# Issuing every engine in source order from the third token chunk on, in a one-core attention and feed-forward kernel

## The chip, the cores and the metric

The kernel runs on one core of a Trainium2 chip. The metric is the device time of one launch in microseconds. Four compute engines work beside each other: PE (matrix products), DVE (vector), ACT (scalar functions and scaled copies) and POOL (a second, slower vector engine). SP starts the DMA transfers. Each engine executes its own instruction list in order, and semaphores join the lists.

## The reference

Linear attention with random features for 8 batches of 576 tokens and 8 heads, then a feed-forward layer on the 4608 tokens that come out:

```python
def _attn_ref(q, k, v, omega):
    m, D = omega.shape                       # 128 features, head_dim 64
    scale = 1.0 / np.sqrt(np.sqrt(D))
    q_s, k_s = (q * scale, k * scale)
    def phi(x):
        proj = np.einsum('bhsd,md->bhsm', x, omega)
        sq = np.sum(x * x, axis=-1, keepdims=True) / 2.0
        h = proj - sq
        h = h - np.max(h, axis=-1, keepdims=True)
        return np.exp(h) / np.sqrt(m)
    q_p, k_p = (phi(q_s), phi(k_s))
    kv = np.einsum('bhsm,bhsd->bhmd', k_p, v)
    z = np.sum(k_p, axis=2)
    num = np.einsum('bhsm,bhmd->bhsd', q_p, kv)
    den = np.einsum('bhsm,bhm->bhs', q_p, z)[..., None] + 1e-06
    return num / den

def _moe_ref(x, w_in, w_out):                # x 4608x512, w_in 512x2048, w_out 2048x512
    h = x @ w_in
    sp = np.where(h > 20.0, h, np.log1p(np.exp(np.minimum(h, 20.0))))
    g = h * np.tanh(sp)                      # Mish
    return g @ w_out
```

## The kernel before

**Numbers.** Nearly every factor is held as two fp16 parts, the rounded value (hi) and what is left of it (lo), and a product is three products: lo·hi, hi·lo and hi·hi. The function cast makes hi, mostly on ACT (L72), and the function rest makes lo, on DVE (L81, L83) or POOL (L81).

**Work.** The 4608 tokens make 18 chunks (c) of 256. Three kinds of work stand beside each other:

- *The feed-forward layer.* ff_in(c) forms h = x·w_in in PSUM (tile ph, L689), eight steps ("i") of 24 matmuls 128x256. ACT applies Mish (L834), ACT makes hi of g and DVE lo (L83). ff_out(c-1) forms g·w_out (tile po, L858), eight steps ("o") of 12 matmuls 128x512. ACT copies po to the tile o, and SP stores it.
- *Query units,* two a chunk (q_task): SP loads fq. ACT makes hi of it (tile sq) and POOL lo. PE projects it (pq, L340). DVE takes the maximum and subtracts it (mxq L349, eq L358). ACT applies Exp and makes hi of qn, and DVE lo. SP transposes qn to qp. PE multiplies by kv (pn, L495), DVE divides (rd, x) and casts (xs), POOL makes lo of xs, and SP transposes xs into the chunk's tile xT, the right factor of ff_in.
- *Key units,* four a batch (k_task): the same as far as Exp, with fk, sk, pk, mxk, ek and kp; then PE multiplies kp by the values vb (pkv, L445). The values of a whole batch are loaded by v_task as four tiles vf. DVE takes their largest magnitude (vmx L278), which scales them.

The functions of ACT lie in two tables, one for Exp and one for Mish. Each change of function is an ACT_TABLE_LOAD.

**Chunks 15 to 17** (SC0 = 15) use seven block products in place of eight (ff_in7). Four of the seven left factors are sums of blocks of w_in (s1 to s4). The function s_make forms them ahead of that, once for each of four quarter pairs ("sets"): DVE adds fp16 blocks into an fp32 tile s (L724), ACT makes hi (L72), DVE lo (L81), and SP writes the pair to DRAM. ff_in7 loads them back (w<-ds), and DVE joins the products (L801).

**Order.** A step counter (slot) drives generators. From chunk 2 on a slot is one "i" or one "o" step of the feed-forward layer, followed by whatever the agenda has due: each `yield n` in a unit sets it back by n slots. Chunk c begins at slot 65 + 16(c-2). Units start by the hand list FIRST (18 entries) and then by pace(c), a linear rule. The source order made in this way isn't what the engines execute: a scheduler orders each engine's list by its own model, and an instruction written late may stand early. The sets start at slots 211, 222, 233 and 244 and take eight slots each.

**Buffers** that the prediction speaks of: three xT tiles, two xs, five vf, five ht (the h tiles and the tile s of s_make).

Of the kernel before, what the change touches and what calls it, by code (L numbers as in the profile page):

```python
# [9 lines left out]
F16 = mybir.dt.float16  # L10
# [20 lines left out]
def tile_kernel(  # L31
# [58 lines left out]

    idle = const.tile([P, 512], F16, name="idle")
    dve.memset(idle, 1.0)
# [34 lines left out]
    def pow2(amax, tag, top):  # L127


        allm = over_partitions(amax, tag)  # L130
# [12 lines left out]

    NB = 8
    BW = KT * DF // NB
    wo_t = const.tile([P, NB, 2, BW], F16, name="wo")
    slots = [const.tile([P, 2, BW], F16, name=f"w{i}") for i in range(NB + 1)]
    slots += [wo_t[:, i] for i in range(NB)]
    def flat32(slot):
# [121 lines left out]
    def v_task(b):  # L271
# [117 lines left out]
    def k_task(nth, b, hp):  # L389
# [75 lines left out]
    def q_task(nth, t):  # L465
        c, off = t * P // CH, t * P % CH
        if c not in xT:
            xT[c] = sb.tile([P, 2, KT, CH], F16, tag="xT", name=f"xT{c}", bufs=3)
        rows = slice(0, P)
# [13 lines left out]
        )  # L483
        yield 2
        x = sb.tile([P, H, D], F32, tag="x", name=f"x{t}", bufs=2)
# [31 lines left out]

    x_more = {}

    def x_region(c, r):  # L520

        n = (4, 4, 4, 2)[r]
        if r < 2:
            return xT[c].rearrange("p a k s -> p (a k s)")[:, r * 1024:(r + 1) * 1024].rearrange(
                "p (a k s) -> p a k s", a=2, k=n
            )
        if (c, r) not in x_more:
            x_more[c, r] = sb.tile([P, 2, n, P], F16, tag="vf", name=f"xm{c}_{r}", bufs=5)
# [36 lines left out]
    def x_parts(nth, t, x):  # L565
        c, off = t * P // CH, t * P % CH
        if c >= SC0:
            yield from x_sums(nth, t, x)
            return
        xs = sb.tile([P, 2, H * D], F16, tag="xs", name=f"xs{t}", bufs=2)  # L570
# [4 lines left out]
        nc.sync.dma_start_transpose(  # L575
            out=xT[c].rearrange("p a k s -> p (a k) s")[:, :, off:off + P],
            in_=xs.rearrange("p a c -> p (a c)"),
        )
        did("x", c)
# [90 lines left out]
    def ff_in(c):  # L670
# [3 lines left out]
        for gr in range(FT // FG):  # L674
            gT[c, gr] = sb.tile([P, 2, FG, CH], F16, tag="g", name=f"g{c}_{gr}", bufs=GB)
            for q in range(FG // FQ):
# [4 lines left out]
                for j in range(0, FQ, 2):  # L681
                    ph = ps_h.tile([P, 2, CH], F32, tag="h", name=f"ph{c}_{gr}_{q}_{j}")
                    for i in range(2):
# [4 lines left out]
                        for n, (a, y, k) in enumerate(mm):  # L688
                            nc.tensor.matmul(  # L689
                                out=ph[:, i, :], lhsT=wi(a, k, f) if c else wi0(k, f),  # L690
                                rhs=xT[c][:, y, k, :] if c else xT0()[:, k, :],
                                start=n == 0, stop=n == len(mm) - 1,
# [16 lines left out]

    SUMS = ("s2", "s3", "s1", "s4")  # L710
    sums = {}
# [4 lines left out]
    def s_make(gr, hb):  # L716
# [18 lines left out]
        tt(s, s, u, ALU.add)  # L735
        send("s1", s)
        yield 2
        tt(s, s, block(sl1, 0, 0))
        tt(s, s, block(sl1, 1, 0))
        send("s2", s)  # L740
        yield 2
        tt(u, block(sl1, 0, 1), s)
        tt(u, u, block(sl1, 1, 1), ALU.add)
        send("s4", u)
        yield 2
# [3 lines left out]
        send("s3", s)  # L749
        did("sums")  # L750
# [15 lines left out]
    def ff_in7(c):  # L766
# [18 lines left out]

        def products(gr, op_l, op_r):
            r, k0 = right[op_r]
            mm = [(a, y, k) for a, y in ((1, 0), (0, 1), (0, 0)) for k in range(2)]
            ph = ps_a.tile([P, FQ, P], F32, tag="a", name=f"p_{op_l}_{c}_{gr}")
            for i in range(FQ):  # L790
                for n, (a, y, k) in enumerate(mm):
                    nc.tensor.matmul(  # L792
                        out=ph[:, i, :], lhsT=left(gr, op_l, i, a, k), rhs=x_region(c, r)[:, y, k0 + k, :],
                        start=n == 0, stop=n == len(mm) - 1,
                    )
            if op_l in SUMS:
                ask_sum()
            return ph

        def add(out, in0, bank):  # L800
            dve.tensor_tensor(out=out, in0=bank, in1=in0, op=ALU.add)  # L801

        for gr in range(FT // FG):
# [4 lines left out]

            p1 = products(gr, "a11", "b11")
            cast(act, c21, p1)  # L810
            yield
            add(c11, c21, products(gr, "a12", "b21"))
            yield
            add(c12, c21, products(gr, "s2", "t2"))
            yield
            add(c21, c12, products(gr, "s3", "t3"))
            yield
            p5 = products(gr, "s1", "t1")
            add(c22, c21, p5)
            add(c12, c12, p5)  # L820
            yield
            add(c12, c12, products(gr, "s4", "b22"))
            later(1, mish, sp, h[0], h[0])
            later(2, g_split, c, gr, 0, sp, h[0])
            yield
            add(c21, c21, products(gr, "a22", "t4"))
            later(1, mish, sp, h[1], h[1])
            later(2, g_split, c, gr, 1, sp, h[1])
            yield

# [89 lines left out]

    def pace(c):

        return 15 + (c - 1) * 4.0 if c < 5 else 31.0 + (c - 5) * 3.8

# [37 lines left out]

    items, need = [], {}
    nb = 0
    for t in range(NT):
        last = (t * P + P - 1) // S
        while nb <= last:
            items += [("k", nb, hp) for hp in range(HP)]
            nb += 1
        items.append(("q", t))  # L970
        need[t * P // CH] = len(items)
    given = [0]

    def give():
        if given[0] < len(items):
            it = items[given[0]]
            given[0] += 1
            start((k_task if it[0] == "k" else q_task)(given[0] - 1, *it[1:]))
            if it[0] == "k" and it[2] == HP - 1 and it[1] + 1 < B:
                start(v_task(it[1] + 1), V1)  # L980

    w_in_v = w_in.rearrange("(k p) f -> p k f", p=P)
# [14 lines left out]
    for what in PREL.split():  # L997
# [58 lines left out]
    while agenda:  # L1056
        step()


# [39 lines left out]
```

## Time and profile before

Three runs took 983.06, 964.0 and 962.81 us, a median of 964.0 us.

| | |
|---|---|
| profiled execution: time | 962.69 us |
| its span | 960.8 us |
| mean granted TensorE clock | 0.992 |
| busy PE, ACT, DVE, POOL over the span | 98%, 66%, 65%, 23% |
| 192 to 264 us: PE busy of 72 us | 70.84 |
| 264 to 624 us: PE, ACT, DVE busy of 360 us | 359.57, 263.90, 219.69 |
| 624 to 768 us (sets of s_make): PE, ACT, DVE busy of 144 us | 140.03, 111.36, 121.17 |
| 816 to 936 us (seven products): PE, ACT, DVE busy of 120 us | 120.00, 37.88, 50.91 |

In the profile's lines an instruction is `start us, length us, engine, line, operation, out<-in, shape, xcount`, and a bracket holds the idle time ahead of it and what ended that. Lengths on one engine overlap a little: the next instruction can begin shortly before the end of the last. Chunk 2 begins near 190 us. The first 190 us load and split the weights, and the last 24 us are the last chunk's output product.

### The profile page before, as it was taken

The numbers are of one execution on the slowest core, as the hardware profiler recorded it, in microseconds if no ns is written. First come the engines' busy times: TensorE is split into PE (matmuls) and PEld (weight loads), VectorE is DVE, ScalarE is ACT, GpSimd is POOL, SyncE is SP. The second block draws the span as 40 slices with busy tenths as digits, with TensorE's granted clock in tenths as the row PEclk, the third lists the DMA queues.
The fourth block names the chain that finished last, engine by engine and source line by source line (L and its number), as shares of the span: only waits on it lengthen the run. The fifth ranks groups of instructions, "written<-read, shape, count | busy, mean of one in ns | idle before, by whom it ended". The sixth has DMA issues, their size and how long they took to land. (4 is left out here: it accounts for less than half of the span.)

```text
span 960.8 us, 20397 instructions
## 1 busy us (share of the span) xinstructions
PE 940.9 (98%) x8568; PEld 679.3 (71%) x8568; DVE 624.9 (65%) x1080; ACT 633.9 (66%) x818; POOL 222.7 (23%) x141
## 2 busy tenths in 40 slices
PE   9999988999999999999999999999989999999998
PEld 6788873677677777777777777777756777777663
DVE  5879797587766666656575655788889656643330
ACT  4758875686877877768667775778776866332231
POOL 0000052242432322322133333222231332200000
PEclk9979999999999999999999999999999999999999
DMA  9866314431741346313431253423552145634410
GB/s 287 271 208 208 109 48 94 102 58 61 140 92 37 107 77 119 69 59 75 101 68 53 69 118 66 93 89 68 136 124 73 37 100 115 172 117 131 133 57 33
DMA packets 147403, 100.25 MB, mean 104 GB/s; under 512 B 112112, under 2 KB 124528, under 8 KB 147312
## 3 DMA queue, kind: packets, MB, share of 16 engines
q1 hardware_dynamic: 147312, 98.95, 41.2%
q8 instruction: 67, 1.10, 0.5%
q14 instruction: 24, 0.20, 0.1%
HBM read 58.95 MB, written 13.63 MB: 76 GB/s over the span
## 5 line engine op out<-in xcount | busy, mean ns | idle before, releaser
L858 PE MATMUL po<-wo,g 128*128 128x512 f16 x1632 | 375.2, 380 | 0.0
L689 PE MATMUL ph<-xT,w 128*128 128x256 f16 (+1 forms) x2816 | 344.8, 279 | 0.7 <-ACT xT L72 0.7
L689 PEld LDWEIGHTS <-w 128*128 128x128 f16 x2688 | 261.0, 98 | 47.3 <-issue 0.7
L858 PEld LDWEIGHTS <-g 128*128 128x128 f16 x1632 | 155.1, 98 | 163.9 <-issue 2.2
L83 DVE SCALAR_TENSOR_TENSOR g<-h,us,g 128x1024 f16<-128x1024 f32 (+3 forms) x92 | 120.2, 1316 | 36.8 <-ACT g L72 36.2
L834 ACT ACTIVATE h<-ph,us 128x512 f32<-128x512 f32 (+3 forms) x152 | 83.3, 573 | 77.6 <-PE ph L689 76.8
L81 POOL TENSOR_TENSOR sq<-fq,sq 64x1024 f16<-64x1024 f32 x31 | 69.0, 2227 | 159.1 <-issue 65.2
L81 POOL TENSOR_TENSOR sk<-fk,sk 64x1152 f16<-64x1152 f32 x24 | 60.5, 2520 | 111.5 <-ACT sk L72 86.9
L81 POOL TENSOR_TENSOR xs<-x,xs 128x512 f16<-128x512 f32 (+1 forms) x35 | 44.2, 1264 | 151.9 <-issue 68.0
L72 ACT ACTIVATE g<-h,us 128x1024 f16<-128x1024 f32 (+3 forms) x80 | 72.6, 932 | 1.2
L834 ACT ACT_TABLE_LOAD x55 | 70.6, 1283 | 1.0
L364 ACT ACT_TABLE_LOAD x53 | 68.0, 1283 | 4.2 <-DVE ek L358 3.3
L349 DVE TENSOR_REDUCE mxq<-pq 128x4 f32<-128x512 f32 x72 | 46.8, 682 | 31.7 <-PE pq L340 31.6
L792 PEld LDWEIGHTS <-w 128*128 128x128 f16 x1008 | 58.4, 98 | 5.9
L81 DVE TENSOR_TENSOR qn<-eq,qn 128x1024 f16<-128x1024 f32 x31 | 38.9, 1254 | 36.2 <-ACT qn L72 36.2
L349 DVE TENSOR_REDUCE mxk<-pk 128x4 f32<-128x512 f32 (+1 forms) x96 | 50.1, 548 | 18.0 <-PE pk L340 18.0
L834 ACT ACTIVATE h<-h,us 128x1024 f32<-128x1024 f32 (+2 forms) x16 | 14.7, 933 | 61.9 <-DVE h L801 61.9
L72 ACT ACTIVATE o<-po,us 128x512 f32<-128x512 f32 (+1 forms) x38 | 25.8, 680 | 40.1 <-PE po L858 40.0
L81 DVE TENSOR_TENSOR kp<-ek,kp 128x1152 f16<-128x1152 f32 x24 | 36.4, 1515 | 24.0 <-ACT kp L72 24.0
L364 ACT ACTIVATE eq<-eq,lnt 128x1024 f32<-128x1024 f32 x31 | 35.6, 1148 | 21.2 <-DVE eq L358 21.0
L81 POOL TENSOR_TENSOR vb<-vf,vb 128x640 f16<-128x640 f32 x24 | 39.4, 1641 | 40.6 <-DVE vb L74 28.7
L801 DVE TENSOR_TENSOR h<-p_s,h 128x512 f32<-128x512 f32 x30 | 20.2, 689 | 43.2 <-PE p_s L792 43.2
(140 smaller groups left out, 1156.9 us busy)
## 6 DMA issues: line engine op xcount, KB each, us to landing
w<-ds SPq DMA_DIRECT2D x48, 256.0 KB, 3.4
vf<-in_vL_dram SPq DMA_DIRECT2D x32, 325.0 KB, 3.3
fq<-in_qT_dram SPq DMA_DIRECT2D x36, 256.0 KB, 3.6
out_dram<-o SPq DMA_DIRECT2D x36, 256.0 KB, 2.3
fk<-in_kT_dram SPq DMA_DIRECT2D x24, 256.0 KB, 3.6
raw<-in_w_out_dram SPq DMA_DIRECT2D x5, 1024.0 KB, 8.9
wo<-in_w_in_dram SPq DMA_DIRECT2D x4, 1024.0 KB, 13.2
raw<-in_w_in_dram SPq DMA_DIRECT2D x4, 1024.0 KB, 15.2
```

The costliest lines, as they stand in the source:

```text
L72: act.activation(out, in_, AF.Copy, scale=scale)
L81: eng.tensor_tensor(out=out, in0=in_, in1=hi, op=ALU.subtract)
L83: eng.scalar_tensor_tensor(out=out, in0=in_, scalar=scale, in1=hi, op0=ALU.mult, op1=ALU.subtract)
L349: sub = dve.tensor_reduce(out=mx[:, lo:hi], in_=pp[:, :m, :], axis=AX.X, op=ALU.max, negate=by_act)
L364: last = act.activation(e, e, AF.Exp, bias=lnt)
L689: nc.tensor.matmul(out=ph[:, i, :], lhsT=wi(a, k, f) if c else wi0(k, f), rhs=xT[c][:, y, k, :] if c else xT0()[:, k, :], start=n == 0, st ...
L792: nc.tensor.matmul(out=ph[:, i, :], lhsT=left(gr, op_l, i, a, k), rhs=x_region(c, r)[:, y, k0 + k, :], start=n == 0, stop=n == len(mm) - 1,)
L801: dve.tensor_tensor(out=out, in0=bank, in1=in0, op=ALU.add)
L834: act.activation(h[:, :, lo:hi], ph[:, :, lo:hi], AF.Mish, scale=us[:, 0:1])
L858: nc.tensor.matmul(out=po[i], lhsT=gT[c, gr][:, a, f % FG, i * P:(i + 1) * P], rhs=wo(y, f), start=f == 0 and (a, y) == parts[0], stop=f = ...
```

## The change

**Order.** From chunk 2 on, `tc.manual_schedule` keeps the source order on PE, SP, DVE, ACT and POOL. Units begin at slots that are computed: query units 27 and 23 slots ahead of their chunk, key units backward from there at slot 1 or 13 of a chunk. The hand list still starts the first 21 units. From unit 17 on a key unit's product stands four slots after its casts (KV_GAP) and a query unit's pn three after its transpose (QP_GAP).

**Values** are loaded and reduced one tile at a time (v_unit), each started from the key unit ahead of it.

**x tiles.** A chunk has one tile of 3584 columns that holds either the plain x or all four regions of the seven-product form; there are two of them in place of three xT. The tiles xs are three in place of two, and ht is four in place of five.

**s_make** has a slot between a sum, its cast and its rest. It takes 12 slots for each set, and the sets start 12 slots apart (209, 221, 233, 245).

**ff_in7** has four steps for each half in place of seven. Products that are added to one another are chained in a PSUM bank (pa), which ACT copies out on the way, so that DVE adds three banks for each half. Chunks 15 to 17 run "io" eight times like the others.

```diff
+    def v_unit(b, hp):
+        if hp == 0:
+            vstate[b] = ({}, None, None)
...
+        vstate[b][0][hp] = t = fetch_v(b, hp)
+        yield 4
+        dve.tensor_reduce(
+            out=vm[b][:, hp:hp + 1], in_=t[:, :, 0:D], axis=AX.XY, op=ALU.max, apply_absolute_value=True
+        )
...
-        yield gap("kv", f"k{b}_{hp}")
+        if b > 1 and b + 1 < B and hp + 1 < HP:
+            start(v_unit(b + 1, hp + 1), 2)
+        yield KV_GAP if nth >= LATE else gap("kv", f"k{b}_{hp}")
...
-            xT[c] = sb.tile([P, 2, KT, CH], F16, tag="xT", name=f"xT{c}", bufs=3)
...
+            xT[c] = sb.tile([P, 3584], F16, tag="xT", name=f"xT{c}", bufs=2)
...
         def send(op, src):
-            o = sb.tile([P, 2, n], F16, tag="xs", name=f"{op}_{gr}_{hb}", bufs=2)
+            o = sb.tile([P, 2, n], F16, tag="xs", name=f"{op}_{gr}_{hb}", bufs=3)
             cast(act, o[:, 0], src)
+            yield 1
             rest(dve, o[:, 1], src, o[:, 0])
+            yield 1
             sums[gr, hb, op] = dram.tile([P, 2, n], F16, name=f"d{op}_{gr}_{hb}")
             nc.sync.dma_start(out=sums[gr, hb, op], in_=o)
...
-        send("s1", s)
-        yield 2
+        yield from send("s1", s)
+        yield 1
...
-    GB, HB, QB = 4, 5, 1
+    GB, HB, QB = 4, 4, 1
...
-    FIRST = (0, 1, 2, 3, 4, 4, 9, 9, 19, 21, 24, 27, 32, 36, 43, 58, 59, 68)
+    FIRST = (0, 1, 2, 3, 4, 4, 9, 9, 19, 21, 24, 27, 32, 36, 43, 58, 59, 62, 65, 68, 71)
...
+    LATE, KV_GAP, QP_GAP = 17, 4, 3
...
+    for it in items[F:]:
+        if it[0] == "q":
+            base[it] = CS(it[1] // 2) - (23 if it[1] % 2 else 27)
...
-        at(slot[0] + 16 * (SC0 - 6) + 2 + 11 * i, lambda i=i: start(s_make(i // 2, i % 2)))
+        at(slot[0] + 16 * (SC0 - 6) + 12 * i, lambda i=i: start(s_make(i // 2, i % 2)))
+    own = ExitStack()
+    own.enter_context(tc.manual_schedule(engines={mybir.EngineType.PE, mybir.EngineType.SP, mybir.EngineType.DVE, mybir.EngineType.Activation, mybir.EngineType.Pool}))
...
-        order = "io" * 8 if c < SC0 else "iioiioioioi" * 2
+        order = "io" * 8
         for j, what in enumerate(order):
-            if j % 2 == 0 and given[0] < min(pace(c + j / len(order)), len(items)):
+            while F <= given[0] < len(items) and begin[given[0]] <= slot[0]:
                 give()
             next(fi if what == "i" else fo, None)
-            if (j + 1) * 16 // len(order) > j * 16 // len(order):
-                step()
+            step()
```

Three places show how the lists move. The first is SP's list in chunk 2, before the change, from the transpose of query unit 8's qn (qp8) on. fq9 is the load of query unit 9, xT4 the tile of chunk 4, and vf3_1 the second value tile of batch 3:

```order
L481 DMA_TRANSPOSE qp8_1707<-qn8_1654 128x16x128
L575 DMA_TRANSPOSE xT3_1266<-xs7_1789 128x8x128
L297 DMA fq9_2024<-in_qT_dram 64x1024
L575 DMA_TRANSPOSE xT4_1497<-xs8_1868 128x8x128
L297 DMA fq10_2258<-in_qT_dram 64x1024
```

The same place after:

```order
L600 DMA_TRANSPOSE xT3_1486<-xs7_1827 128x8x128
L600 DMA_TRANSPOSE xT4_1946<-xs8_1907 128x8x128
L271 DMA vf3_1_1957<-in_vL_dram 128x650
L320 DMA fq9_2001<-in_qT_dram 64x1024
L271 DMA vf3_2_2085<-in_vL_dram 128x650
L931 DMA out_dram<-o1_0_2147 128x512
L328 DMA fk3_0_2205<-in_kT_dram 64x2x512
```

The load of fq9 stood ahead of the transpose into xT4 and now stands behind it, with a value tile between them.

The second place is ACT's list around the first set's s1 and s2, before:

```order
L72 ACTIVATE kp6_1_7531<-ek6_1_7420 128x1152
L72 ACTIVATE s1_0_0_7543<-s0_0_7539 128x512
L834 ACT_TABLE_LOAD
L834 ACTIVATE h11_0_0_7393<-ph11_0_0_2_7503,us4_6150 128x2x64
L834 ACTIVATE h11_0_0_7393<-ph11_0_0_2_7503,us5_7387 128x2x192
L72 ACTIVATE g11_0_7392<-h11_0_0_7393,us4_6150 128x4x64
L72 ACTIVATE g11_0_7392<-h11_0_0_7393,us5_7387 128x4x192
L72 ACTIVATE s2_0_0_7619<-s0_0_7539 128x512
```

And after (Mish is the line with h<-ph, Exp the one with lnt):

```order
L72 ACTIVATE o9_1_7380<-po9_1_6719,us4_6038 128x512
L72 ACTIVATE s1_0_0_7386<-s0_0_7382 128x512
L387 ACT_TABLE_LOAD
L387 ACTIVATE eq25_7318<-eq25_7318,lnt_72 128x1024
L72 ACTIVATE qn25_7403<-eq25_7318 128x1024
L875 ACT_TABLE_LOAD
L875 ACTIVATE h11_0_0_7345<-ph11_0_0_0_7346,us4_6038 128x2x64
L875 ACTIVATE h11_0_0_7345<-ph11_0_0_0_7346,us5_7339 128x2x192
L72 ACTIVATE s2_0_0_7517<-s0_0_7382 128x512
L875 ACTIVATE h11_0_0_7345<-ph11_0_0_2_7413,us4_6038 128x2x64
```

The cast of s1 stood behind a key unit's Exp and its cast; now it stands ahead of a query unit's table load and Exp. The cast of s2 stood behind the Mish and the casts of one h tile; now it stands between that tile's two Mish pairs.

The third place is DVE's list around s4, before:

```order
L724 TENSOR_TENSOR s0_0_7539<-s0_0_7539,w0_106 128x512
L358 TENSOR_TENSOR ek6_2_7590<-pk6_2_5_7604,mxk6_2_7591 128x512
L724 TENSOR_TENSOR s0_0_7539<-w0_106,w2_108 128x512
L81 TENSOR_TENSOR s4_0_0_7712<-s0_0_7539,s4_0_0_7712 128x512
L74 CAST vb1_120<-vf6_3_6613 128x10x64
```

And after (rd25 to xs25 are the division and cast of query unit 25):

```order
L81 TENSOR_TENSOR kp6_2_7575<-ek6_2_7492,kp6_2_7575 128x1152
L749 TENSOR_TENSOR s0_0_7382<-w0_75,s0_0_7382 128x512
L749 TENSOR_TENSOR s0_0_7382<-s0_0_7382,w0_75 128x512
L529 TENSOR_SCALAR rd25_7612<-pn25_0_7613 128x4
L533 RECIPROCAL rd25_7612<-rd25_7612 128x4
L534 TENSOR_TENSOR x25_7611<-pn25_0_7613,rd25_7612 128x256
L529 TENSOR_SCALAR rd25_7612<-pn25_1_7626 128x4
L533 RECIPROCAL rd25_7612<-rd25_7612 128x4
L534 TENSOR_TENSOR x25_7611<-pn25_1_7626,rd25_7612 128x256
L74 CAST xs25_7663<-x25_7611 128x512
L81 TENSOR_TENSOR s4_0_0_7643<-s0_0_7382,s4_0_0_7643 128x512
```

The additions for s4 lay among a key unit's subtractions; now both stand between that unit's last step on DVE and the division that empties the banks pn of query unit 25.

More of the change, by code (lines that the diff above doesn't have):

```diff
@@ L88, in tile_kernel @@
     dve.memset(lnt, LNT)
-    idle = const.tile([P, 512], F16, name="idle")
+    NB = 8
+    BW = KT * DF // NB
+    wo_t = const.tile([P, NB, 2, BW], F16, name="wo")
+    slots = [const.tile([P, 2, BW], F16, name=f"w{i}") for i in range(NB + 1)]
+    slots += [wo_t[:, i] for i in range(NB)]
+    idle = slots[NB][:, 0, 0:512]
     dve.memset(idle, 1.0)
@@ L136, in pow2 @@
         return top_over(p, tag, top)
[L144 to L148, printed above, removed]
     def flat32(slot):
@@ L287, in v_task @@
         vstate[b] = (vt, p, s)
+    def v_unit(b, hp):
+        if hp == 0:
+            vstate[b] = ({}, None, None)
+            vm[b] = sb.tile([P, HP], F32, tag="vmx", name=f"vmx{b}", bufs=2)
+        vstate[b][0][hp] = t = fetch_v(b, hp)
[3 more added lines that the diff above has]
+        )
+        if hp < HP - 1:
+            return
+        am = sb.tile([P, 1], F32, tag="vam", name=f"vam{b}")
+        dve.tensor_reduce(out=am, in_=vm[b], axis=AX.X, op=ALU.max)
+        allm = over_partitions(am, f"v{b}")
+        yield 1
+        p, s = pow2_of(allm, f"v{b}", TOP)
+        vstate[b] = (vstate[b][0], p, s)
+    vm = {}
     kv = {}
@@ L735, in s_make @@
         tt(s, s, u, ALU.add)
[L736 to L737 removed]
+        yield from send("s1", s)
+        yield 1
         tt(s, s, block(sl1, 0, 0))
         tt(s, s, block(sl1, 1, 0))
[L740 to L741 removed]
+        yield from send("s2", s)
+        yield 1
         tt(u, block(sl1, 0, 1), s)
         tt(u, u, block(sl1, 1, 1), ALU.add)
[L744 to L745 removed]
+        yield from send("s4", u)
+        yield 1
         tt(s, block(sl1, 0, 0), block(sl2, 0, 0))
@@ L748, in s_make @@
         tt(s, s, u, ALU.add)
-        send("s3", s)
+        yield from send("s3", s)
         did("sums")
@@ L784, in left, with products @@
             return sl[:, a, o:o + P]
-        def products(gr, op_l, op_r):
+        def products(bank, gr, op_l, op_r, first):
             r, k0 = right[op_r]
             mm = [(a, y, k) for a, y in ((1, 0), (0, 1), (0, 0)) for k in range(2)]
-            ph = ps_a.tile([P, FQ, P], F32, tag="a", name=f"p_{op_l}_{c}_{gr}")
             for i in range(FQ):
@@ L792, in products, with bank, add @@
                     nc.tensor.matmul(
-                        out=ph[:, i, :], lhsT=left(gr, op_l, i, a, k), rhs=x_region(c, r)[:, y, k0 + k, :],
-                        start=n == 0, stop=n == len(mm) - 1,
+                        out=bank[:, i, :], lhsT=left(gr, op_l, i, a, k), rhs=x_region(c, r)[:, y, k0 + k, :],
+                        start=first and i == 0 and n == 0, stop=n == len(mm) - 1, skip_group_check=True,
                     )
             if op_l in SUMS:
[L797 to L801, printed above, removed]
+                later(1, ask_sum)
+        def bank(pool_, tag, name):
+            return pool_.tile([P, FQ, P], F32, tag=tag, name=name)
+        def add(out, bank):
+            dve.tensor_tensor(out=out, in0=bank, in1=out, op=ALU.add)
         for gr in range(FT // FG):
@@ L806, in ff_in7, with mish7 @@
             c11, c12, c21, c22 = (x[:, :, o:o + P] for x in h for o in (0, P))
-            p1 = products(gr, "a11", "b11")
-            cast(act, c21, p1)
+            pa = bank(ps_h, "h", f"pa{c}_{gr}")
+            products(pa, gr, "a11", "b11", True)
+            cast(act, c11, pa)
+            pb = bank(ps_a, "a", f"pb{c}_{gr}")
+            products(pb, gr, "a12", "b21", True)
+            later(1, add, c11, pb)
             yield
-            add(c11, c21, products(gr, "a12", "b21"))
+            products(pa, gr, "s2", "t2", False)
+            cast(act, c12, pa)
+            pd = bank(ps_h, "h", f"pd{c}_{gr}")
+            products(pd, gr, "s1", "t1", True)
             yield
-            add(c12, c21, products(gr, "s2", "t2"))
+            products(pa, gr, "s3", "t3", False)
+            cast(act, c22, pa)
+            later(1, add, c22, pd)
             yield
-            add(c21, c12, products(gr, "s3", "t3"))
-            yield
[L818 to L829, printed above, removed]
+            products(pa, gr, "a22", "t4", False)
+            mish7(sp, h[1], pa)
+            products(pd, gr, "s4", "b22", False)
+            later(1, add, c12, pd)
+            later(1, mish, sp, h[0], h[0])
+            later(2, g_split, c, gr, 1, sp, h[1])
+            later(3, g_split, c, gr, 0, sp, h[0])
+            yield
+    def mish7(sp, h, pa):
+        for us, lo, hi in sp:
+            if lo < P:
+                e = min(hi, P)
+                act.activation(h[:, :, lo:e], pa[:, :, lo:e], AF.Mish, scale=us[:, 0:1])
+            if hi > P:
+                b = max(lo, P)
+                act.activation(h[:, :, b:hi], h[:, :, b:hi], AF.Mish, scale=us[:, 0:1])
     def mish(sp, h, ph):
@@ L961, in step @@
         slot[0] += 1
[L963 to L971, printed above, removed]
+    items = [("q", t) for t in range(NT)] + [("k", b, hp) for b in range(B) for hp in range(HP)]
+    items.sort(key=lambda it: it[1] if it[0] == "q" else it[1] * S // P - 0.5)
+    F = len(FIRST)
+    base = {}
+    for it in items[F:]:
+        if it[0] == "q":
+            base[it] = CS(it[1] // 2) - (23 if it[1] % 2 else 27)
+    late = CS(NCH)
+    for it in reversed(items[F:]):
+        if it[0] == "k":
+            late = min(late, base["q", it[1] * S // P]) - 1
+            while (late - CS(0)) % 16 not in (1, 13):
+                late -= 1
+            base[it] = late
+    items[F:] = sorted(items[F:], key=lambda it: base[it])
+    begin = list(FIRST) + [base[it] for it in items[F:]]
     given = [0]
@@ L1057, in tile_kernel @@
         step()
+    own.close()
 def kernel(**inputs):
```

46 lines of the change are left out of this document (24 added, 22 removed).

## The prediction

> **What bounds the kernel now.** I read the page's busy shares first, then busy time by stretch (columns: stretch, length, PE, PEld, DVE, ACT, POOL busy, clock, DMA share, GB/s), then PE's waits from 190 us on, where the changed order begins (us in total, times, longest).
>
> ```profile
> span 960.8 us, 20397 instructions
> PE 940.9 (98%) x8568; PEld 679.3 (71%) x8568; DVE 624.9 (65%) x1080; ACT 633.9 (66%) x818; POOL 222.7 (23%) x141
> 264.00:624.00 360.00, 359.57 (x3438) 259.25 (x3436) 219.69 (x394) 263.90 (x296) 109.31 (x60) 1.00 0.38 80
> 624.00:768.00 144.00, 140.03 (x1296) 99.45 (x1294) 121.17 (x194) 111.36 (x146) 38.15 (x22) 0.99 0.35 88
> 816.00:936.00 120.00, 120.00 (x1345) 85.91 (x1344) 50.91 (x81) 37.88 (x48) 5.19 (x5) 1.00 0.42 123
> PE pk L340 <- DVE x L511: 2.7, 2, 2.4
> PE pkv L445 <- DVE kp L81: 1.9, 2, 1.5
> PE pn L495 <- DMA qp<-qn: 0.9, 1, 0.9
> ```
>
> PE is the bound. From chunk 2 on its matmuls are the same ones in the same number, so an order can win only PE's waits: 2.7 + 1.9 + 0.9 = 5.5 us. One more thing can come back, in the timeline of the sets of sums:
>
> ```profile
> 698.32 2.75 PE L858 MATMUL po<-wo,g 128*128 128x512 f16 x12
> 706.63 0.63 PE L340 MATMUL pk<-om,sk 128*128 128x128 f16 x8 [2.38 <-DVE x L511]
> 707.08 4.44 PE L858 MATMUL po<-wo,g 128*128 128x512 f16 x12
> 742.78 1.13 PE L445 MATMUL pkv<-vb,kp 128*128 128x65 f16 x30 [1.50 <-DVE kp L81]
> ```
>
> After the wait of 2.38 us the next twelve matmuls took 4.44 us where others took 2.75: 1.7 us more. The wait of 1.50 us had no such row behind it. So at most 5.5 + 1.7 = 7.2 us can go: of the profiled execution's 962.7 us (960.8 span and 1.9 around it) 955.5 us stay. The runs' median is 964.0, 1.3 above that execution, which I take as it is. A measurement of this kernel tells about 2%, 19 us, from no change, so faster by that isn't to be had from order.
>
> **The change part by part.**
>
> *Plain stretch (264 to 624 us).* PE waits next to nothing in 360 us before, so there is nothing to win, and the question is whether a fixed order adds waits. Four slots of PE are two steps "i", two steps "o" and a pk or pq with a pkv or pn:
>
> ```profile
> 767.61 0.96 PE pkv L445 x30
> 751.74 1.00 PE pk L340 x18
> 768.57 2.62 PE ph L689 x24
> 771.19 2.59 PE po L858 x12
> ```
>
> That is 2 x 2.62 + 2 x 2.59 + 1.00 + 0.96 = 12.4 us, with pq and pn 0.3 less; I use 12.2. In it DVE works 219.69 / 360 = 61% of the time and ACT 73%, so each has over 3 us left. The longest chain that must fit in the four slots of KV_GAP is the key unit's:
>
> ```profile
> 317.56 0.88 DVE L349 TENSOR_REDUCE mxk<-pk 128x4 f32<-128x512 f32 x2
> 319.87 0.69 DVE L358 TENSOR_TENSOR ek<-pk,mxk 128x512 f32<-128x512 f32 x1
> 328.54 1.28 ACT L364 ACT_TABLE_LOAD   x1
> 308.19 1.25 ACT L364 ACTIVATE ek<-ek,lnt 128x1152 f32<-128x1152 f32 x1
> 309.51 1.15 ACT L72 ACTIVATE kp<-ek 128x1152 f16<-128x1152 f32 x1
> 323.10 1.36 DVE L81 TENSOR_TENSOR kp<-ek,kp 128x1152 f16<-128x1152 f32 x1 [0.76 <-ACT kp L72]
> 326.90 0.69 ACT L834 ACTIVATE h<-ph,us 128x512 f32<-128x512 f32 x1
> 334.44 1.15 ACT L72 ACTIVATE g<-h,us 128x1024 f16<-128x1024 f32 x1
> ```
>
> The maxima and subtractions reach from 317.56 to 320.56, 3.0 us. 3.0 + 1.28 + 1.25 + 1.15 + 1.36 = 8.0 us, and a Mish and a g cast ahead of it on ACT (0.69 + 1.15) make 9.9. That fits with 2.3 to spare: zero. Single value tiles, the third xs, ht at four and the moved idle tile lie under the same cover and cost nothing.
>
> *Two x tiles.* In chunk 2 SP's transpose into xT4 must now wait until PE has read xT2 for the last time. Query unit 8 still begins by the hand list (slot 59), so its transpose comes up in slot 73, and chunk 2's last "i" is slot 79. Behind it on SP stand vf3_1 and fq9, and pq of unit 9 is due on PE in slot 80, behind that slot's "o". Before, fq9 was ahead of the transpose. The chain from the end of the "i" in slot 79:
>
> ```profile
> 255.81 1.24 SPq L575 DMA_TRANSPOSE xT<-xs  x1
> 215.00 0.36 SPq L268 DMA_DIRECT2D vf<-in_vL_dram  x1
> fq<-in_qT_dram SPq DMA_DIRECT2D x36, 256.0 KB, 3.6
> 327.47 1.05 ACT L72 ACTIVATE sq<-fq 64x1024 f16<-64x1024 f32 x1
> L81 POOL TENSOR_TENSOR sq<-fq,sq 64x1024 f16<-64x1024 f32 x31 | 69.0, 2227 | 159.1 <-issue 65.2
> ```
>
> 1.24 + 0.36 + 3.6 + 1.05 + 2.23 = 8.5 us, less the 2.59 us of the "o" meanwhile: PE stands 5.9 us, once. DVE waits in its list for vf3_1 meanwhile, a shorter chain. (Elsewhere a late value tile, its cover gone, would cost such a load, about 3.6 us.) Bounds: 0 if SP passes the transpose earlier than I count, 5.9 + 1.7 if the clock drops as at 707.08. I take 5.9. Every later query unit begins 27 or 23 slots ahead of its chunk and comes to its transpose 5 slots after the tile was read: zero. The Trainium skill, "TensorE: Matmul & The Clock Gate", section "What's actually happening", halves PE's clock after an idle window of about 3.4 us. By that rule the wait costs 1.7 more and the sum ends near 980. The row at 707.08 shows the drop already behind 2.38 us, and that at 742.78 none behind 1.50.
>
> *The sets of sums* are where DVE has least room: 121.17 of 144 us, 84%, before. The work stays, but the places are now fixed, and three of them stand in chains that PE waits for. Rows, the tile s by operation first (min/median/max ns):
>
> ```profile
> L724 DVE TENSOR_TENSOR s<-s,w x12: 674/684/1909, 630.0 to 730.7; 128x512 f32<-128x512 f32 x12
> L72 ACT ACTIVATE s<-s x16: 612/630/632, 626.1 to 741.6; 128x512 f16<-128x512 f32 x16
> L81 DVE TENSOR_TENSOR s<-s,s x16: 675/684/2205, 627.5 to 742.6; 128x512 f16<-128x512 f32 x16
> 302.94 0.83 ACT L434 ACTIVATE vf<-vf,s_v 128x640 f32<-128x640 f32 x1 [0.79 <-DVE s_v L124]
> 335.99 0.82 DVE L278 TENSOR_REDUCE vmx<-vf 128x1 f32<-128x640 f32 x1 [2.22 <-DMA vf<-in_vL_dram]
> 336.73 1.27 DVE L83 SCALAR_TENSOR_TENSOR g<-h,us,g 128x1024 f16<-128x1024 f32 x1
> 715.09 0.15 DVE L506 TENSOR_SCALAR rd<-pn 128x4 f32<-128x4 f32 x1
> 715.27 0.18 DVE L510 RECIPROCAL rd<-rd 128x4 f32<-128x4 f32 x1
> 715.48 0.42 DVE L511 TENSOR_TENSOR x<-pn,rd 128x256 f32<-128x256 f32 x1
> ```
>
> I add these up by hand from 0, where PE starts the slot of s1, each length less the 0.08 by which neighbours overlap.
> - s1: DVE is through with the pq unit at 2.0, vmx 2.75, g 3.95, three additions 5.75. ACT: cast of s1 6.4, table 7.7, Exp 8.95, cast 10.1. DVE: qn's lo 11.4, half a division 12.1. It empties the bank that PE's next pk wants at 11.7: 0.4 late.
> - s2 and s4: DVE: the other half and xs 13.2, two additions 14.4. ACT: cast of s2 15.05, Mish 15.75, sk 16.8, g 17.95, table 19.2, Exp 20.5, kp 21.65, vf 22.5. DVE: vb 23.0, kp's lo 24.3, two additions for s4 25.5, half a division 26.2. PE wants the bank at 24.3: 1.9 late.
> - s3: the other half, xs, the lo of s4 27.9, a pk unit 30.7, g 31.9, three additions 33.7. ACT: cast of s3 34.3, table 35.6, Exp 36.85, kp 38.0, vf 38.8, table 40.1, Mish 40.8. PE has used both banks ph at 38.85: 1.95 late.
>
> Together 4.25 a set, 17 us for four. Below: before, PE waited 2.7 + 1.9 = 4.6 us in the sets' stretch, and zero is possible. Above: a DVE instruction with a long neighbour on POOL:
>
> ```profile
> 700.70 2.37 POOL L81 TENSOR_TENSOR sk<-fk,sk 64x1152 f16<-64x1152 f32 x1 [5.46 <-ACT sk L72]
> 701.41 2.21 DVE L81 TENSOR_TENSOR s<-s,s 128x512 f16<-128x512 f32 x1
> ```
>
> This lo of s took 2.21 us where the median is 0.684, 1.53 more, and ended half a microsecond after POOL. Two such in a set's three late chains cost 3.1 a set, 12.2 in all. I take 17: the ledger goes by ordinary lengths. The Trainium skill, "SBUF — State Buffer", section "Who interferes with whom", says the same of the pair: a DVE instruction with two SBUF inputs is fully blocked while a GpSimd instruction that reads SBUF holds the shared port. Its rule would send the sum to 990; it is the first rival.
>
> *Seven products.* DVE adds fewer banks, ACT copies more; PE is at 120.00 of 120 us there and its products are the same: zero, covered by DVE's 50.91 and ACT's 37.88 of 120.
>
> The sum: 962.7 - 7.2 + 5.9 + 17 = 978.4, so 978.
>
> **The rivals.**
> - *Slower: DVE blocked beside POOL in the sets.* In the fixed order POOL's sk, sq and xs start behind the same ACT casts that let DVE's sums start, so they meet in each set. 978.4 + 12.2 = 990.6; with a drop of the clock (1.7) in each set 997. It decides from the fourth blocked instruction on (983.3 is 2% above 964.0; 4.9 / 1.53 = 3.2). For it: the maxima near 2 us in the rows of s. Against: the medians there are ordinary, and PE can take up what falls into another chain's slack.
> - *Absorbed.* The ledger starts each set with nothing in hand; if units are a slot early when a set begins, 3 us of slack covers the sets. 955.5 + 5.9 = 961.4; with the sets' waits and the drop as before (4.6 + 1.7), 967.7. For it: with DVE at 84% PE lost only 4.6 us there before. Against: the scheduler moved sums out of the way then, as the order shows.
> - *The change doesn't do what it says:* the first 21 units stay on the hand list. That is the 5.9 us above; if they are early enough after all and the sets are absorbed too, 955.5.
>
> **How the numbers follow.** Forecast 0.36 (970 to 983), blocked 0.30 (983 to 997 and beyond), absorbed 0.32 (956 to 969), all gone 0.02. Within 2%: 0.36 + 0.32 + 0.01 = 0.69; slower 0.30; faster 0.01, for what the floor of 955.5 excludes unless its count is wrong. The range of 956 to 997 leaves out the 0.02 and some 0.08 above. The forecast's own range is 970 to 983.
>
> **What would show it.** In PE's waits after: one of about 6 us for sq of POOL (or ACT) in chunk 2, near 235 us; and in four stretches 36 us long from about 630 us on, waits for x of DVE at a pk (0.4 and 1.9) and for Mish at a ph (2). If PE is 99% busy from 630 to 780 us, the ledger is wrong and the sets are absorbed; if lo and additions of s have medians above 1 us, the blocking decides. A wait in the plain stretch would show that its slack was counted too high, and one from 816 us on that the chained products cost something.

## The result, and the profile after

The changed kernel takes 1021.9 us (median) where the kernel before takes 964.2: a ratio of 1.062, interval 1.054 to 1.071. That is slower by 58 us and 25 us above the range's upper end.

In some executions of the kernels here, the profiled one of the changed kernel (1033.4 us) among them, PE is granted only half clock from about 18 to 55 us and the whole takes 17 to 21 us longer, as the stretch from 24 to 60 us shows, before and after (columns: stretch, length, busy PE, PEld, DVE, ACT, POOL, clock, DMA share, GB/s):

```profile
24.00:60.00 36.00, 33.63 (x213) 29.58 (x213) 30.74 (x53) 19.21 (x48) 0.35 (x1) 0.86 0.79 259
```

```profile
24.00:60.00 36.00, 35.75 (x164) 31.92 (x164) 15.68 (x26) 16.20 (x39) 0.00 (x0) 0.56 0.55 182
```

PE's matmuls are the same in number in all kernels, so I compare when PE starts its n-th one in two traces. What has been lost by its 1350th matmul (204.3 us before, 222.1 after: 17.8 us) is the start. From there on the changed kernel loses 53.2 us. Without what the start lost the profiled execution comes to 1033.4 - 17.8 = about 1016 us, and from here on a time in brackets, (1016), is that of a profiled execution so corrected. The changed kernel's four executions without a profile took 1020.5 to 1022.4; no trace shows where their other 5 us lie, and that stays open.

| lost against the kernel before, us | seam, matmul 1350 to 1950 | plain, to 5400 | sets, to 6900 | rest | sum |
|---|---|---|---|---|---|
| the changed kernel | 11.2 | 11.8 | 31.8 | -1.7 | 53.2 |

The seam is the part of chunk 2 and 3 where the hand list ends and the computed slots begin, and "sets" is most of the stretch of s_make. The boundaries are at 204, 265, 628, 791 and 957 us before. The kernels start units at somewhat different matmuls, so that each column can be off by some 3 us (experiment 3 below has 3.2 us in a plain stretch with one wait of 0.8); the sum is not.

The page of the kernel after, and PE's waits from 190 us on:

```profile
span 1031.6 us, 20316 instructions
PE 971.3 (94%) x8568; PEld 701.8 (68%) x8568; DVE 601.1 (58%) x1056; ACT 642.7 (62%) x838; POOL 235.4 (23%) x141
PE pk L363 <- DVE x L534: 17.1, 6, 5.2
PE pq L363 <- POOL sq L81: 11.2, 4, 4.4
PE pq L363 <- DVE ek L381: 9.3, 1, 9.3
PE ph L714 <- ACT h L875: 7.9, 5, 3.4
```

5.5 us of waits have become 46.3. Nearly all of the 46.3 us lies in three places.

**The seam** (DVE ek, 9.3 us) is the transpose into the third x tile, in the timeline after:

```profile
240.02 1.23 SPq L600 DMA_TRANSPOSE xT<-xs  x1
241.97 0.51 SPq L320 DMA_DIRECT2D fq<-in_qT_dram  x1
244.99 0.82 DVE L299 TENSOR_REDUCE vmx<-vf 128x1 f32<-128x640 f32 x1 [8.16 <-DMA vf<-in_vL_dram]
247.66 2.49 POOL L81 TENSOR_TENSOR sq<-fq,sq 64x1024 f16<-64x1024 f32 x1 [9.57 <-ACT sq L72]
250.99 0.69 DVE L381 TENSOR_TENSOR ek<-pk,mxk 128x512 f32<-128x512 f32 x1
251.83 1.87 PE L363 MATMUL pq<-om,sq 128*128 128x128 f16 x16 [9.29 <-DVE ek L381]
```

SP issues the transpose only when PE has finished chunk 2's last "i" step, as foreseen, and the load of fq9 behind it. sq is ready at 250.15. But DVE stood 8.16 us for the value tile queued behind the same transpose, and everything behind vmx on DVE came later still: the last PSUM bank is empty at 251.7.

**POOL's reduction** (POOL sq, 11.2 us in four waits) wasn't in the sum. In the plain stretch after:

```profile
345.83 0.76 POOL L120 PARTITION_ALL_REDUCE allm_v<-vam  x1 [6.57 <-DVE vam L305]
346.94 0.14 DVE L140 TENSOR_SCALAR p_v<-allm_v 128x1 int32<-128x1 int32 x1
353.41 2.12 POOL L81 TENSOR_TENSOR sq<-fq,sq 64x1024 f16<-64x1024 f32 x1 [6.81 <-issue]
355.58 1.07 PE L363 MATMUL pq<-om,sq 128*128 128x128 f16 x16 [1.75 <-POOL sq L81]
```

From the end of the reduction POOL starts nothing for 6.8 us, though the cast for sq was through at 340.9 and DVE worked with the reduction's result from 346.94 on. The trace of before has the same gap, with nothing urgent behind it:

```profile
301.77 0.38 POOL L114 PARTITION_ALL_REDUCE allm_v<-vam  x1 [6.21 <-DVE g L83]
309.21 2.13 POOL L81 TENSOR_TENSOR sq<-fq,sq 64x1024 f16<-64x1024 f32 x1 [7.07 <-issue]
```

**The sets** (DVE x and ACT h; 22.2 of these 25.0 us lie in the sets). Stretches between the same matmuls of PE (the 1950th to the 5400th, and on to the 6900th), after:

```profile
293.84:668.94 375.10, 367.50 (x3453) 263.76 (x3451) 209.31 (x391) 258.54 (x295) 112.20 (x58) 1.00 0.33 77
668.94:863.82 194.88, 168.99 (x1503) 118.89 (x1501) 137.55 (x224) 125.44 (x159) 48.65 (x26) 0.95 0.30 73
```

195 us for what took 163 before; DVE is busy only 138 of 195. What it looks like at s4 and s3 of the first set, in the timeline:

```profile
679.25 1.89 DVE L749 TENSOR_TENSOR s<-w,s 128x512 f32<-128x512 f16 x1
681.17 0.69 DVE L749 TENSOR_TENSOR s<-s,w 128x512 f32<-128x512 f32 x1
681.89 0.63 ACT L72 ACTIVATE s<-s 128x512 f16<-128x512 f32 x1 [2.21 <-DVE s L749]
682.18 0.42 DVE L534 TENSOR_TENSOR x<-pn,rd 128x256 f32<-128x256 f32 x1
682.66 0.62 PE L363 MATMUL pk<-om,sk 128*128 128x128 f16 x8 [4.24 <-DVE x L534]
683.12 4.45 PE L714 MATMUL ph<-xT,w 128*128 128x256 f16 x24
690.92 0.63 ACT L72 ACTIVATE s<-s 128x512 f16<-128x512 f32 x1 [5.51 <-DVE s L749]
692.86 1.26 ACT L387 ACTIVATE ek<-ek,lnt 128x1152 f32<-128x1152 f32 x1
698.24 2.78 PE L714 MATMUL ph<-xT,w 128*128 128x256 f16 x24 [1.02 <-ACT h L875]
```

The order of events is that of the ledger: the division waits behind s4's additions and PE behind the division, then ACT stands 5.51 us at the cast of s3 with Exp and Mish queued behind it. The view of the tile s says how much that is (who waited for it: us, times):

```profile
  ACT s L72: 45.7, 12
```

**Clock.** The granted clock over the 195 us is 0.95, some 10 us of PE's work. From 190 us on each of the six waits of 3.41 us or more has matmuls at about half speed behind it (682.66 and 683.12 above: 24 in 4.45 us for 2.78), and so has the one of 2.68 us in the plain stretch:

```profile
501.39 1.07 PE L363 MATMUL pq<-om,sq 128*128 128x128 f16 x16 [2.68 <-POOL sq L81]
502.29 4.45 PE L714 MATMUL ph<-xT,w 128*128 128x256 f16 x24
```

The waits of 2.37 us and less have none here, but one of 2.38 us had it before, and one of 2.42 us has it in an experiment below. The Trainium skill, "TensorE: Matmul & The Clock Gate", section "What's actually happening", has the clock fall after an idle window of about 3.4 us. The six long waits agree with that, and the three shorter ones (2.38, 2.42 and 2.68 us) don't; the measurement decides. What tells the short waits apart is worked out in the last section.

### The profile page after: what moved, and what is told of

It is laid out like the page before. It is cut to its first block, busy times and chain, and to the rows that moved or that the text cites. A ratio compares the mean times of both kernels' runs of the same rounds, so it can differ in the third digit from the quotient of the medians.

```text
span 1031.6 us, 20316 instructions
## 1 busy us (share of the span) xinstructions
PE 971.3 (94%) x8568; PEld 701.8 (68%) x8568; DVE 601.1 (58%) x1056; ACT 642.7 (62%) x838; POOL 235.4 (23%) x141
## 5 line engine op out<-in xcount | busy, mean ns | idle before, releaser
L714 PE MATMUL ph<-xT,w 128*128 128x256 f16 (+1 forms) x2816 | 356.2, 285 | 8.6 <-ACT h L875 7.9
L714 PEld LDWEIGHTS <-w 128*128 128x128 f16 x2688 | 266.8, 100 | 56.1 <-issue 9.2
L83 DVE SCALAR_TENSOR_TENSOR g<-h,us,g 128x1024 f16<-128x1024 f32 (+3 forms) x92 | 95.3, 1054 | 24.6 <-ACT g L72 24.1
L372 DVE TENSOR_REDUCE mxq<-pq 128x4 f32<-128x512 f32 x72 | 49.2, 685 | 80.3 <-PE pq L363 80.2
L81 POOL TENSOR_TENSOR vb<-vf,vb 128x640 f16<-128x640 f32 x24 | 51.6, 2151 | 125.7 <-DVE vb L74 125.6
L81 POOL TENSOR_TENSOR sk<-fk,sk 64x1152 f16<-64x1152 f32 x24 | 58.0, 2415 | 92.6 <-ACT sk L72 83.8
L818 PEld LDWEIGHTS <-w 128*128 128x128 f16 x1008 | 58.2, 98 | 5.8 <-DMA w<-ds 0.7
L363 PE MATMUL pq<-om,sq 128*128 128x128 f16 x496 | 34.4, 225 | 23.6 <-POOL sq L81 14.3
L387 ACT ACTIVATE ek<-ek,lnt 128x1152 f32<-128x1152 f32 x24 | 30.2, 1257 | 40.9 <-DVE ek L381 40.8
L363 PEld LDWEIGHTS <-sq 128*128 128x128 f16 x496 | 31.2, 101 | 32.1 <-POOL sq L81 16.6
L72 ACT ACTIVATE s<-s 128x512 f16<-128x512 f32 x16 | 10.1, 630 | 60.6 <-DVE s L749 45.7
```

What stands on the lines that cost most here:

```text
L72: act.activation(out, in_, AF.Copy, scale=scale)
L81: eng.tensor_tensor(out=out, in0=in_, in1=hi, op=ALU.subtract)
L83: eng.scalar_tensor_tensor(out=out, in0=in_, scalar=scale, in1=hi, op0=ALU.mult, op1=ALU.subtract)
L363: nc.tensor.matmul(out=pp[rows, i, :], lhsT=left[:, o:o + rows.stop - rows.start], rhs=right, start=j == 0, stop=j == len(terms) - 1,)
L372: sub = dve.tensor_reduce(out=mx[:, lo:hi], in_=pp[:, :m, :], axis=AX.X, op=ALU.max, negate=by_act)
L387: last = act.activation(e, e, AF.Exp, bias=lnt)
```

## The experiments

Each is the changed kernel with one edit, unless it says otherwise. Losses are counted as above.

**1. Query unit 8 later.**

```diff
-    FIRST = (..., 43, 58, 59, 62, 65, 68, 71)
+    FIRST = (..., 43, 58, 62, 65, 68, 70, 71)
...
-    LATE, KV_GAP, QP_GAP = 17, 4, 3
+    LATE, KV_GAP, QP_GAP = 16, 4, 3
...
+    items.insert(F - 2, items.pop(items.index(("q", 8))))
```

> Query unit 8 begins at slot 70 in place of 59 (the three key units beside it keep their slots), so that its transpose into the third x tile comes up after PE has read the first; nothing else is changed. If the wait of SP at that transpose is what stopped PE at 251.83 us (9.29 us idle, 14.5 us lost against the kernel before between 229 and 275 us), no wait of PE over 2 us is left in chunk 2, and the time falls by 12 to 15 us, to about 1007 to 1010. Rival: units that stand close together at the seam of hand list and grid hold DVE and ACT up whatever SP does; then a wait of 5 us or more stays there and the time is above 1015.

1031.8 us (1014). The 9.3 us wait is gone, but PE then waits 2.2 and 2.4 us for DVE at units that stand three slots apart: the seam costs 7.3 in place of 11.2. Between theory and rival.

**2. Only the transpose later.**

```diff
         rest(by("xlo", nth), xs[:, 1], xf, xs[:, 0])
-        yield 1
+        yield 8 if t == 8 else 1
```

> The changed kernel with only that transpose seven slots later. Moving the whole unit left 7 us lost at the seam, as its neighbours then stood three slots apart. Theory: the wait at the transpose alone is worth the 12 to 14 us lost between 229 and 275 us; no wait of PE over 2 us is left in chunk 2. Rival: 5 us or more of waits stay there, for crowded units.

1012.1 us (1012); the seam costs 4.9 in place of 11.2, and the longest wait there is 1.6 us. So the transpose is worth 6 to 8 us at the seam. In the whole only 4 come out of it: the waits for sq that follow are 2.01, 2.49 and 3.01 us for 1.75, 2.68 and 2.37, two of them with the clock drop behind in place of one.

**3. POOL's reduction two slots later,** behind the query unit's sq.

```diff
         if hp < HP - 1:
             return
+        yield 2
         am = sb.tile([P, 1], F32, tag="vam", name=f"vam{b}")
```

> The largest magnitude of a batch of values is joined over the partitions on POOL two slots later, behind the query unit's lo part in place of ahead of it; nothing else is changed. Theory: after each such reduction POOL issues nothing for about 7 us (6.81 at 353.41, 7.01 at 711.98), and in the fixed order sq stands right behind it. Then the waits of PE for sq of POOL (1.75, 2.68, 2.37 and 4.44 us from 190 us on) go, and the time falls by 11 to 14 us to about 1008 to 1011. Rival: sq is late because its load or its cast on ACT is late, and POOL merely looks idle; then those waits stay and the time is 1018 or more.

1006.9 us (1006). All waits for sq of POOL are gone from 190 us on and the plain stretch costs 3.2 in place of 11.8. The sets still cost 31.5 of 31.8: the wait for sq there went too (4.44 us), but those for x and Mish grew. The theory holds, a little below its 11 to 14 us: the reduction costs about 9 us by what stands behind it.

**4. Sums spread** over chunks 6 to 13, into slots without a division or a lo part, the tile s with a buffer of its own, ht at three.

```diff
-        at(slot[0] + 16 * (SC0 - 6) + 12 * i, ...start(s_make...))
+        at(CS(6) + 10 + 32 * i, ...start(s_make...))
```

> The block sums are made over chunks 6 to 13, a set in 32 slots, in slots where DVE has neither a division nor a lo part; the tile s has a buffer of its own, and ht is three. Theory: the fixed places of the sums in chunks 11 to 13 cost what is lost between 655 and 803 us (32 us more than before, plus the 6 us that before loses there itself, less 5 us that belong to POOL's reduction). The waits of pk for x and of ph for Mish go, and the time falls by 28 to 33 us to about 988 to 994. Rival: the units of those chunks are late for another reason (in-order DVE and ACT have no room); then waits for x and Mish stay, and the time is above 1005.

1004.3 us (985), the stretch of the sets -1.2 in place of 31.8. The theory holds.

**5. The three together.**

> The three edits together. If the three mechanisms are independent and are all there is, 1021.4 - 14 - 12 - 31 = 964, and with a start like that of the kernel before some 4 us less: 957 to 968, within 1% of the kernel before. Rival: source order costs more than these three places, and 975 or more remains.

972.3 to 974.3 us (973), 1.0085 of before (1.0051 to 1.0119), above the 957 to 968 expected. The sets are 5.0 better than before, the plain stretch costs 2.6, but the seam 14.2: the reduction of batch 3, two slots later, stands right ahead of a key unit's sk (6.1 us of PE). A mend in one place was a new wait in the next.

**6. The three, the seam mended as in 2 and batch 3's reduction left in place.**

> As the three edits together, but the seam in chunk 2 is mended in another way: query unit 8 keeps its start at slot 59 and only its transpose into the third x tile is issued seven slots later, when PE has read the first; and the reduction of batch 3 keeps its place, since two slots later it stood ahead of a key unit's sk (6.1 us of PE). Theory: what the three edits together still lost in chunk 2 (7.5 us at crowded units, 7 us behind the reduction) goes; 972.3 - 14.5 = 958, 956 to 962, a little below the kernel before (963 to 967). Rival: the units crowded at the seam are late in any case; then 5 us or more of waits stay there and the time is 964 to 972.

961.9 to 964.9 us (962), 0.9998 of before (0.9987 to 1.0008): the whole loss is gone, and counted from the 1350th matmul on it is 0.8 us faster than the kernel before.

**7. s4 and s3 one slot later,** additions and casts.

```diff
         yield from send("s2", s)
-        yield 1
+        yield 2
```

> The changed kernel with s4 and s3 of each set one slot later: the additions for s4 then stand behind the division of the same slot in place of ahead of it, and the cast of s3 behind a key unit's Exp burst on ACT. No instruction is added or taken away. Theory (the ledger of the prediction): the waits of PE for x behind s4 (4.24, 3.70, 5.23 us) and for Mish behind s3 (1.02, 3.41, 2.21 us) are these two places; they fall below 1 us each, and the time falls by 18 to 26 us. Rival: DVE is simply full in these chunks, or blocked beside POOL; then the waits move to the next reader and the time falls by less than 8 us.

1009.4 us (1006): 10 us less, the sets 20.6 in place of 31.8. That is between theory and rival, nearer to the rival: the waits for x fell only from 17.1 to 13.1 and those for Mish from 7.9 to 4.9. Ahead of the same matmuls of PE two waits for x fell (4.24 to 1.70, 3.70 to 2.33), the longest stayed (5.23, now 5.30 at 785.46), and one for Mish grew from 0.29 to 2.40. So the place of s4 ahead of the division isn't the heart of it.

**8. The scheduler's order,** all else as changed.

```diff
-    own.enter_context(tc.manual_schedule(engines={...}))
```

> The changed kernel without the command to keep source order: the scheduler orders each engine's list, as before the change, with the units' new places, the two x tiles, the single value tiles and the chained products kept. Theory: source order is what costs; the time is within 2% of the kernel before, 955 to 980. Rival: two x tiles and the new places cost in any order; then 990 or more.

959.1 us (959), 0.995 of before (0.9933 to 0.9966), and PE's waits from 190 us on are one line:

```profile
PE pk L363 <- DVE x L534: 3.1, 4, 1.7
```

Source order is the whole loss, and the rest of the change is worth 5 us.

**9 and 10. DVE alone free; DVE alone fixed.**

> The changed kernel with source order kept on PE, SP, ACT and POOL, and DVE's list alone left to the scheduler. An execution of the changed kernel without a cold start comes to about 1016 us (1033.4 less the 17.5 lost before 60 us). Theory: in the sets DVE's fixed order is what PE pays for (30 us went when the sums were spread); then the waits for x and Mish in the sets fall to a third or less, those for sq of POOL (4 of 2 to 5 us) and the one of 9 us in chunk 2 stay, and the time is 984 to 994. Rival: the casts at their fixed places on ACT hold the chain up as much as DVE does; then it is above 1002.

> The other way round: source order kept on DVE alone, the scheduler orders ACT, POOL and SP (PE's list is the same). Theory: the sets still cost most of their 30 us, since the additions stand where they stood, and what POOL and SP cost goes: 980 to 995. Rival: with ACT and POOL free DVE's order costs little, below 972.

DVE free: 1002.7 us (998), near the rival's time but not for its reason: the sets cost nothing (-0.2), with the casts on ACT where they were. The plain stretch costs 30.2: PE waits there 13.7 us for sq of POOL (6.8 in the changed kernel) and 6.5 for Mish. From 190 us on:

```profile
PE pq L363 <- POOL sq L81: 23.7, 5, 7.4
```

DVE fixed, the others free: 959.1 us (960), the sets -1.1, though every addition and every lo part stands where it stood in DVE's list. I had expected 980 to 995. In its view of s, who waited for it:

```profile
  ACT s L72: 13.5, 12
```

13.5 us in place of 45.7: the scheduler had put the casts of s1 and s3 behind the Exp. With that the ledger's picture of DVE as the full engine falls. For the sets it is enough to free DVE alone, or to free the others.

**11. The kernel before in source order,** nothing else of the change.

> The kernel before with the command to keep source order from chunk 2 on and nothing else of the change: units by the linear rule, values of a batch at once, three x tiles, s_make at its old slots, seven separate products. Theory: source order without places made for it is slower still than the change, since units then stand at slots that fit no pattern: 1030 to 1100. Rival: the new places and the two x tiles are what costs, and source order alone is harmless: below 980.

1058.4 us in the better of two executions, (1056) in the profiled one, with 93.8 us lost after the start: 37.3 us of it in waits of pn for the transpose of qn, 13.9 for Mish. Source order with the rest of the change is better by 40 us than without it.

**12. The scheduler's order with the sums spread.**

> The changed kernel in the scheduler's order (959.1 us) with the sums spread over chunks 6 to 13. In that version PE waits 3.1 us from 190 us on, so at most 3 us can go: 956 to 960. Rival: the spread sums and ht at three tighten other places, 960 to 964.

959.9 us (960), 0.995 (0.9934 to 0.9967): nothing beyond 8. PE's floor is near.

**13. The casts of the sums one slot later.** The lo parts on DVE come a slot later with them; the additions and the stores keep their slots.

```diff
+            yield 1
             cast(act, o[:, 0], src)
             yield 1
             rest(dve, o[:, 1], src, o[:, 0])
-            yield 1
```

> The changed kernel with every cast of a sum one slot later on ACT; the additions keep their places on DVE, the order of PE is the same. The casts of s1 and s3 then stand behind the Exp burst and the Mish that they stood ahead of, that of s2 behind a Mish pair; that of s4 stays ahead of one. In the changed kernel ACT stood 45.7 us before these casts, waiting for the additions (12 times), with Exp and Mish queued behind; with DVE alone in fixed order and ACT free it was 13.5 us, and nothing was lost. Theory: the fixed places of the casts on ACT are what hold the chain in the sets: the time falls by 15 to 25 us from about 1016, to 991 to 1001. Rival: the places of the additions on DVE do; less than 8 us.

986.3 us (984), 32 less than (1016). The sets cost 1.2 in place of 31.8, with the additions where they were. In the view of s and among PE's waits:

```profile
  ACT s L72: 9.9, 5
```

```profile
PE pk L363 <- DVE x L534: 4.2, 2, 2.4
PE ph L714 <- ACT h L875: 0.9, 1, 0.9
```

This settles the sets: the casts stood ahead of an Exp burst or a Mish on ACT and waited there for DVE. One slot later three of the four in a set stand behind what they had held up, and ACT waits 9.9 us ahead of them in place of 45.7. The lo parts that moved with them aren't it: in 10 they kept their places in DVE's list, and nothing was lost. Behind s4's additions, which still stand ahead of a division on DVE, one wait and the half clock remain, in the timeline:

```profile
663.56 0.62 PE L363 MATMUL pk<-om,sk 128*128 128x128 f16 x8 [2.42 <-DVE x L534]
664.01 4.45 PE L714 MATMUL ph<-xT,w 128*128 128x256 f16 x24
```

**14, 15, 16. ACT alone, POOL alone, SP alone fixed.**

> Source order on ACT alone; the scheduler orders DVE, POOL and SP (PE's list is the same in all of these). Theory: ACT's fixed casts wait only where DVE's additions are late, and a free DVE takes them early: 960 to 975. Rival: ACT's list in source order stops Exp and Mish by itself: 980 or more.

> Source order on POOL alone. With only DVE free (ACT, POOL and SP fixed) PE waited 23.7 us for sq of POOL. Theory: the reduction stands ahead of sq on POOL at five places, and each costs 2 to 7 us whatever the others do: 970 to 985. Rival: with SP and ACT free the query loads and casts come early enough, and POOL's order alone costs under 4 us: 959 to 963.

> Source order on SP alone. Theory: the only place where its order costs is the transpose into the third x tile, with the loads behind it: 6 to 12 us, 965 to 972. Rival: with the other engines free the loads queued behind it are not yet needed: 957 to 961.

ACT: 990.0 us (971), 8.6 us lost after the start, 4.0 of them in the sets; as expected. POOL: 966 to 969 us (969), 6.5 us lost, but no wait for sq of POOL is left; the loss lies in waits for x and Mish, so neither theory nor rival had the reason. SP: 994.0 us (987), 24.4 lost after the start, far more than foreseen:

```profile
PE pk L363 <- DVE x L534: 16.5, 10, 3.8
PE pq L363 <- POOL sq L81: 2.7, 1, 2.7
PE pa L818 <- DMA w<-ds: 2.5, 1, 2.5
```

The loads and transposes keep the rhythm of the slots while the other lists no longer do; that this is the cause isn't shown, and why DVE's divisions are late at ten places stays open.

**17. The smallest mends of the three places,** those of 2, 3 (from batch 4 on) and 13 together, source order on all engines.

> Source order on all engines with the smallest mends of the three places: the casts of the sums one slot later (worth 29.5 us by the run before), POOL's reduction two slots later from batch 4 on, the transpose of query unit 8 seven slots later. Theory: these three places are all that source order costs here; 1016 - 29.5 - 10 - 10 = 966 in an execution without a cold start, 961 to 968, the same as the kernel before within 0.5%. Rival: what is queued at one place was hidden behind another, and 972 or more remains.

964.7 to 969.3 us (966), 1.0033 of before (1.001 to 1.0055); 3.7 us lost after the start, of 53.2. The three places add up to nearly all of it.

## Why the prediction was wrong

*What bounds the kernel: right.* PE's floor of 955.5 us holds; the best versions reach 959.

*Seven products at zero: right.* The rest is -1.7 us.

*Plain stretch at zero: wrong, by 11.8 us.* The step that failed is the zero itself, taken from one chain: "the longest chain that must fit in the four slots of KV_GAP is the key unit's". That chain counted DVE and ACT and left out POOL, which is busy 23% of the time and makes the query unit's sq. The waits for sq there are 6.8 us, one for x 0.8 and the half clock behind the wait of 2.68 us 1.7; the rest is within the 3 us of the column. The row that was needed stood in the trace of before (309.21, 7.07 us of "issue" behind the reduction); a busy share doesn't show such a gap. Experiment 3 takes 9 us of it away.

*Two x tiles at 5.9: right in its mechanism, the size was off.* The wait was 9.29 us, and with the clock behind it the seam costs 11.2. Two things make the 3.4 us of difference, half each. The chain from the end of the "i" to sq took 10.2 us (239.95 to 250.15) for the 8.5 of the sum, most of it between the issue of fq9's load and ACT's cast (4.5 for 3.6). And "DVE waits in its list for vf3_1 meanwhile, a shorter chain" failed: it is shorter to vmx, but what DVE had queued behind vmx ended 1.5 us after sq. The bound of 5.9 + 1.7 was too low for the same reasons.

*The sets at 17: right in its mechanism, the size was off by almost half.* PE's waits for x and Mish in the sets are 22.2 us against the ledger's 17; a wait for sq adds 4.4 and the clock some 10; less the 5.6 that the kernel before had lost there, that is about the 31.8 measured. Three things were missing. The ledger priced the clock at nothing, after quoting the row that shows it. It went by ordinary lengths: in the stretch of the sets 15 DVE instructions ran over 0.3 us longer than the median of their line, tile and shape, 16.7 us together (1.89 at 679.25 above). And it named DVE as the engine with least room, where the casts in ACT's list decided (10 and 13).

*The rival with DVE blocked beside POOL* gave 990 to 997. Long DVE instructions beside POOL exist, but counted in the same way the kernel before has 18.1 us of them in the same stretch, in 15 instructions too, and PE lost little there; experiment 13 has 8.5 and 10 has 15.6, and both lose next to nothing. They don't decide.

*"Absorbed"* (0.32) fell with these. The point made against it, that the scheduler had moved sums out of the way, was the right one: what it moves in 10 is the casts.

*The range* ended at 997, since each term had its own upper bound from rows, but PE's waits for sq of POOL, which no term named, had none, and the clock drop was taken once per set in a rival and nowhere in the sum.

## What to carry to other kernels

In a fixed order the costly instruction is a cheap one that waits at the head of a list: 16 casts of 0.63 us cost some 30 us, and one slot later 1 us. Before fixing an engine's order, look at each instruction there whose input comes from another engine in the same slot, and ask what is queued behind it. Busy shares don't show gaps after an instruction: read the idle time ahead of the next one.

## What the runs showed of the hardware

- After PARTITION_ALL_REDUCE on POOL the next tensor instruction starts about 7 us later (6.81, 7.01, 7.07 us with nothing to wait for), and in neither kernel's trace earlier than 6.7 us, though DVE has the reduction's result at once (346.94 above).
- In the trace after, PE's clock falls to half at 246.65, 502.65, 683.56, 714.28, 745.00, 775.72 and 806.44 us: apart by 75, 53 and four times 9 steps of 3.41 us. Laid on such steps, every trace here that has falls (17) shows from 190 us to near its end: a step at full clock in which PE stood idle for 2.02 us or more always had half clock behind it, one with 1.81 us or less never, and between them it went both ways.
- So the length of a wait alone doesn't tell. That of 2.68 us had 2.15 of them in one step, and the clock fell; that of 2.37 us (600.99 to 603.36) was split into 0.65 and 1.72 by a step's end, one of 3.19 us in the run with ACT alone fixed into 1.50 and 1.69, and neither had a fall.
